# One copy of the late decays in DRAM, q and k in two 40-row transfers, narrow fillers and a new order: an mLSTM and two MoE layers on one core

## The chip, the core and the metric

The program runs on one core of a Trainium2 chip. The core has a matrix engine (TensorE: PE in the profile, its weight loads PEld), a vector engine (VectorE, DVE), an activation engine (ScalarE, ACT), a general engine (GpSimd, POOL) and a queue engine (SyncE, SP) that mostly issues DMA transfers. Each engine works through its own list of instructions in order; semaphores tie the lists together. The metric is device time in microseconds (us), the median of 3 runs.

## The reference

```python
for t in range(S):                                   # B=2, H=8, S=768, D=40
    m_new  = np.maximum(f_gate[:, :, t] + m, i_gate[:, :, t])
    f_stab = np.exp(f_gate[:, :, t] + m - m_new)
    i_stab = np.exp(i_gate[:, :, t] - m_new)
    C = f_stab * C + i_stab * outer(v_t, k_t)        # 40x40 a head
    n = f_stab * n + i_stab * k_t
    y[:, :, t] = sigmoid(o_gate_t) * (C @ q_t) / np.maximum(np.abs(n @ q_t), 1.0)
x = y as 1536 tokens of 320
xn = x / rms(x) * rms_g
x = ((silu(xn @ w_gate)) * (xn @ w_val)) @ w_out     # d_ff 1536
h = x @ w_in                                         # d_ff 2048
out = (h * np.clip(h + 3, 0, 6) / 6) @ w_out
```

## The kernel before, in words

The recurrence runs in 6 chunks of 128 steps, two halves of 64 each, for both batches at once. A chunk gives 256 tokens; two chunks make one of three groups of 512 tokens, and both MoE layers run group by group. Every matrix product of the MoE is made of split operands (a high and a low part, both fp32r), so weights are converted on the core first.

The program is written as generators of small steps, and the string `PLAN` (L774) names the order in which steps are put down: `k1.0` is a step of the load of chunk 1, batch 0; a word that comes again is the next step of the same work. Each engine's list is the order in which `PLAN` reaches its steps. The words that matter here:

- `L`, `G`, `g`: load the gates, their scans (`gates_a`), and what is made of them (`gates_b`), in two parts: chunks 0 and 1, and chunks 2 to 5.
- `B`, `b`, `d`: the decays of a chunk, spread over 128 partitions. For chunks 0 to 2 `B` does it on PE (L361, tile `fps`). For chunks 3 to 5 (the "late" ones) `gates_a` writes the decays to DRAM (tile `fsd`, L302), and `b` reads them back with every row going to 64 partitions (`gates_bc`, L347, two transfers of 256 KB a chunk, tile `fbc`). `d` is the scan on DVE (L395) that turns them into a matrix of products, one for each batch. The pool of `fbc` holds two tiles, so chunk 3 is fetched into the tile that chunk 1 frees when its `att` products are done.
- `q`, `k`: load q and k transposed (`rawqk`, L379), and k, v and the output gate (`kvo`, L386).
- `s`, `w`, `a`: scores, their weighting, and `att`, on PE, DVE and PE. `i`, `u`: products with the state, and its update. `l`, `v`, `t`: scaling of k and v, tanh of the gate. `n`, `D`, `e`, `r`: sum, denominator, output and RMS norm of a chunk. `x`: its transposition into the first MoE layer's operand `xT`.
- `W`, `c`: load and conversion of a piece of weights (six steps, spread over ACT, DVE and POOL by the table `ENGINES`). `m`, `M`, `o`: gate product, value product with its DVE and ACT work, and output product of the first MoE layer (tiles `gv` for 256 tokens, `gate` and `val` for 512). `E`, `h`, `p`, `F`: the second layer.
- `H`: a filler, one 128x512 bf16 product of ones whose result nobody reads (`warm_up`, L762).

`ON_DVE` says which of the steps that either DVE or POOL could do are on DVE.

Of the kernel before, what the change touches and what calls it, by code (L numbers as in the profile page):

```python
# [7 lines left out]
F32 = mybir.dt.float32  # L8
# [10 lines left out]
def kernel(  # L19
# [36 lines left out]
    HALF = (0, 64)  # L56
# [29 lines left out]
    hot = ap1.tile([128, 128], mybir.dt.bfloat16, name="hot")  # L86
# [4 lines left out]
    fsd = dram.tile([4, 2 * (NC - 3), BH, LS], F32, name="fsd")  # L91
# [32 lines left out]
    def dma(out, in_, eng=None):  # L124
        (eng or nc.sync).dma_start(out=out, in_=in_)
# [142 lines left out]
    def gates_a(p):  # L268
# [554 lines left out]
    h0.14 h0.15 p0.13 h0.15 h0.15 p0.14 p0.15 h1.0 F0 F0 F0 F0 F0 F0 F0 h1.1 h1.0 F0 h1.0 h1.0 h1.2
# [99 lines left out]
```

## Time and profile before

| | us |
|---|---|
| median of 3 runs | 473.79 |
| runs | 471.18, 473.79, 476.52 |
| the profiled execution, its own time | 476.52 |
| its span in the trace | 474.5 |
| PE busy / DVE busy / ACT busy / POOL busy | 449.0 / 245.2 / 216.0 / 112.4 |

The profiled execution is the slowest of the three runs. Its span is the time from the first to the last instruction in the trace, 2.0 us shorter than the time of the run. Busy PE counts fillers and products at a lowered clock in full, so 95% of busy PE isn't 95% of useful work. The trace is read by stretches below: up to the first product of the MoE at 45.66 us, from there to 148.06 us, where chunk 3 has been transposed and the next gate product starts, and the rest.

### The profile page before, as it was taken

The page shows a single profiled execution, that of the slowest core. Times are in us where ns is not written, and L with a number is a line of the kernel's source. Part 1 is how long each engine was busy: PE and PEld are TensorE (multiplying, and loading weights), DVE is VectorE, ACT ScalarE, POOL GpSimd, SP SyncE. Part 2 cuts the span into 40 slices and gives each one's busy share as a digit, 9 for nine tenths or more (in the row PEclk, how much of TensorE's full clock was granted, in tenths as well). Part 3 has the DMA queues.
Part 4 walks back from the last instruction along what each step waited for, and adds up shares of the span by engine and source line. Part 5 has one row for each costly group of instructions (what it writes and reads, how often), then busy time and mean ns, then how long its engine had stood idle before and what let it go on. Part 6 is the DMA issues. An engine that isn't in the chain of part 4 may idle for free.

```text
span 474.5 us, 9033 instructions
## 1 busy us (share of the span) xinstructions
PE 449.0 (95%) x3823; PEld 380.2 (80%) x3823; DVE 245.2 (52%) x424; ACT 216.0 (46%) x403; POOL 112.4 (24%) x112
## 2 busy tenths in 40 slices
PE   9999929979959999999999999999999999999996
PEld 4766919968848888888887788889998998899985
DVE  4778657767568573251556767863134133232312
ACT  5567736466446232232344537834244234243422
POOL 1515211125212103002151334222232121011311
PEclk9579958999978999999999999999999999999999
DMA  8942761663833010000033334310001000001001
GB/s 262 309 140 92 201 162 63 207 182 108 226 98 140 14 30 15 1 1 1 0 113 110 110 122 153 115 55 1 0 2 55 1 0 1 1 1 55 1 1 55
DMA packets 11024, 38.05 MB, mean 80 GB/s; under 512 B 1768, under 2 KB 3336, under 8 KB 10984
## 3 DMA queue, kind: packets, MB, share of 16 engines
q1 hardware_dynamic: 10408, 36.16, 25.1%
q10 hardware_dynamic: 576, 1.32, 0.8%
q8 instruction: 30, 0.49, 0.5%
q14 instruction: 10, 0.08, 0.1%
HBM read 35.41 MB, written 2.06 MB: 79 GB/s over the span
## 4 chain that ended last, share of the span: by engine, by line
PE 80%; DMA 9%; DVE 5%; ACT 2%; issue 1%; POOL 1%; SPq 0%; DVEq 0%; ACTq 0%
PE hh L593 18%; PE po L600 18%; PE gate L593 9%; PE po L687 9%; PE val L593 8%; DMA fbc<-fsd 7%; PE idle L762 5%; PE gv L593 3%; PE po L690 3%; DMA raw<-in_w_out_dram 2%; PE sc L121 2%; PE fps L361 2%; DVE fbc L395 1%; PE U L121 1%; PE inter L121 1%; PE att L121 1%
## 5 line engine op out<-in xcount | busy, mean ns | idle before, releaser
L593 PE MATMUL hh<-xT,w_in 128*128 128x512 f32 x384 | 89.4, 390 | 0.0
L600 PE MATMUL po<-w_out,g 128*128 128x320 f32 x576 | 86.4, 309 | 0.0
L600 PEld LDWEIGHTS po<-w_out,g 128*128 128x128 f32 x576 | 85.4, 188 | 0.9
L593 PEld LDWEIGHTS hh<-xT,w_in 128*128 128x128 f32 x384 | 71.6, 188 | 14.4
L593 PE MATMUL gate<-xT,w_in 128*128 128x512 f32 x240 | 60.9, 399 | 3.7 <-DVE e L648 2.9
L97 POOL TENSOR_TENSOR g<-r,g 128x512 fp32r<-128x512 f32 x27 | 35.0, 1296 | 123.2 <-ACT g L671 120.0
L668 DVE SCALAR_TENSOR_TENSOR r<-r,hh 128x512 f32<-128x512 f32 x48 | 32.8, 685 | 59.0 <-ACT r L666 59.0
L687 PE MATMUL po<-g,w_out 128*128 128x512 f32 (+1 forms) x252 | 62.6, 377 | 0.1
L593 PE MATMUL val<-xT,w_in 128*128 128x512 f32 x240 | 59.0, 391 | 0.0
L593 PEld LDWEIGHTS gate<-xT,w_in 128*128 128x128 f32 x240 | 45.6, 192 | 14.8 <-DVE e L648 3.3
L671 ACT CAST g<-r 128x512 fp32r<-128x512 f32 x48 | 29.7, 618 | 59.7 <-PE po L600 47.7
L593 PEld LDWEIGHTS val<-xT,w_in 128*128 128x128 f32 x240 | 44.7, 188 | 9.3
L687 PEld LDWEIGHTS po<-g,w_out 128*128 128x128 f32 x252 | 44.9, 198 | 8.0 <-ACT g L652 0.3
L666 ACT ACTIVATE r<-hh,three 128x512 f32<-128x512 f32 x48 | 32.9, 685 | 35.2 <-PE hh L593 26.1
L97 DVE TENSOR_TENSOR g<-r,g 128x512 fp32r<-128x512 f32 x21 | 14.5, 692 | 43.1 <-ACT g L671 43.1
L206 DVE SCALAR_TENSOR_TENSOR raw<-raw,bits 128x640 int32<-128x640 int32 x34 | 32.1, 944 | 5.0 <-ACT raw L200 4.5
L97 POOL TENSOR_TENSOR g<-e,g 128x512 fp32r<-128x512 f32 (+1 forms) x20 | 25.6, 1280 | 38.1 <-ACT g L652 38.1
L593 PEld LDWEIGHTS gv<-xT,w_in 128*128 128x128 f32 x192 | 25.2, 203 | 11.2 <-PE idle L762 9.8
L762 PE MATMUL idle<-hot 128*128 128x512 bf16 x65 | 23.6, 521 | 10.2 <-DVE g L97 9.1
L593 PE MATMUL gv<-xT,w_in 128*128 128x256 f32 x192 | 27.0, 298 | 0.8 <-ACT e L631 0.7
L690 PE MATMUL po<-g,w_out 128*128 128x512 f32 (+1 forms) x84 | 26.4, 368 | 0.0
L631 ACT ACTIVATE e<-gate 128x512 f32<-128x512 f32 x30 | 17.9, 596 | 17.1 <-PE gate L593 16.9
(129 smaller groups left out, 500.2 us busy)
## 6 DMA issues: line engine op xcount, KB each, us to landing
raw<-in_w_out_dram SPq DMA_DIRECT2D x14, 640.0 KB, 4.4
raw<-in_w_gv_dram SPq DMA_DIRECT2D x12, 640.0 KB, 8.4
rawqk<-in_qk_dram SPq DMA_DIRECT2D x12, 448.0 KB, 9.4
raw<-in_w_in_dram SPq DMA_DIRECT2D x8, 640.0 KB, 3.7
kvo<-in_kvo_dram SPq DMA_DIRECT2D x10, 484.0 KB, 4.9
out_dram<-o SPq DMA_DIRECT2D x10, 160.0 KB, 1.9
fbc<-fsd SPq DMA_DIRECT2D x6, 256.0 KB
kvo<-in_kvo_dram ACTq DMA_DIRECT2D x2, 484.0 KB
```

The source lines that it names most:

```text
L97: eng.tensor_tensor(out=out, in0=a, in1=hi.bitcast(F32), op=ALU.subtract)
L121: nc.tensor.matmul(**operands)
L206: nc.vector.scalar_tensor_tensor(out=x, in0=hw, scalar=3, in1=y, op0=ALU.logical_shift_left, op1=ALU.bitwise_or)
L593: nc.tensor.matmul(out=ps, lhsT=w[:, wk], rhs=xT[:, hl, kk], start=(n == 0), stop=(n == len(seq) - 1))
L600: nc.tensor.matmul(out=ps, lhsT=g[:, gh, ts], rhs=w[:, wh, k % 2], start=(first and n == 0), stop=(last and n == 2))
L631: nc.scalar.activation(out=e, in_=pg, func=ACTF.Silu)
L666: nc.scalar.activation(out=r, in_=ps, func=ACTF.Relu, bias=three)
L668: nc.vector.scalar_tensor_tensor(out=r, in0=r, scalar=6.0, in1=ps, op0=ALU.min, op1=ALU.mult)
L671: nc.scalar.copy(out=g[:, 0], in_=r)
L687: nc.tensor.matmul(out=ps, lhsT=w[:, at + n * 128:at + n * 128 + 128], rhs=g[:, gh], start=(first and j == 0), stop=(last and j == 2))
L690: nc.tensor.matmul(out=ps_out[gr, 2][:, ts], lhsT=w[:, 256:DM + 64], rhs=g[:, gh], start=(first and gh == 0), stop=(last and gh == 1))
L762: nc.tensor.matmul(out=idle[i].rearrange("p (a n) -> p a n", n=128), lhsT=hot, rhs=hot.unsqueeze(1).to_broadcast([128, 4, 128]), start=Tru ...
```

## The change

Four edits are made together.

1. `fsd` has one copy of the late decays and no longer four. `gates_a` writes it with one transfer, where it wrote four. `gates_bc` still makes two transfers of 64 rows of 4 KB for each chunk; the source's outermost dimension was the four copies (each read 16 times), and is now 64 repeats of one row.
2. q and k of a chunk and batch come in two transfers of 40 rows (partitions 0 to 39 and 64 to 103), where one transfer brought 112 rows, of which 32 were padding.
3. The fillers' operand `hot` has 2 columns and no longer 128; one column of it is repeated for the weights and for the moving operand.
4. `PLAN`, `ENGINES`, `ON_DVE` and `REM` are new: every step may stand elsewhere. There are 77 fillers, where there were 65. All 77 stand ahead of the first MoE product; before, two stood behind it.

```diff
-    hot = ap1.tile([128, 128], mybir.dt.bfloat16, name="hot")
+    hot = ap1.tile([128, 2], mybir.dt.bfloat16, name="hot")
-    fsd = dram.tile([4, 2 * (NC - 3), BH, LS], F32, name="fsd")
+    fsd = dram.tile([2 * (NC - 3), BH, LS], F32, name="fsd")
...
-    REM = "PAADPA"
+    REM = "APDPPD"
...
-            late_fs = fs[:, (SPREAD - PARTS[p][0]) * L:].rearrange("k (s t) -> k s t", t=LS)
-            for copy in fsd:
-                dma(copy.rearrange("s k t -> k s t"), late_fs)
+            dma(fsd.rearrange("s k t -> k s t"),
+                fs[:, (SPREAD - PARTS[p][0]) * L:].rearrange("k (s t) -> k s t", t=LS))
...
             dma(t[i * LS:(i + 1) * LS].rearrange("p b h t -> p (b h t)"),
-                fsd[:, 2 * (c - SPREAD) + i].rearrange("a k t -> a (k t)").unsqueeze(1)
-                .to_broadcast([4, LS // 4, BH * LS]))
+                fsd[2 * (c - SPREAD) + i].rearrange("k t -> (k t)").partition_broadcast(LS))
...
-        dma(r[0:qk.shape[2]].rearrange("p a h t -> p (a h t)"), qk[c, b])
+        for hh in range(2):
+            dma(r[HALF[hh]:HALF[hh] + D].rearrange("p a h t -> p (a h t)"), qk[c, b, hh])
...
-        nc.tensor.matmul(out=idle[i].rearrange("p (a n) -> p a n", n=128), lhsT=hot, rhs=hot.unsqueeze(1).to_broadcast([128, 4, 128]), start=True, stop=True)
+        nc.tensor.matmul(out=idle[i], lhsT=hot[:, 0:1].to_broadcast([128, 128]),
+                         rhs=hot[:, 0:1].to_broadcast([128, 512]), start=True, stop=True)
...
-    M0.1.0 i1 m0.1.0 c6 a1 M0.1.0 c5 M0.1.0 c6 o0.0.0 M0.1.0 n1.0 b3 n1.1 c5 b3 e1.0 m0.2.0 c6 D1 W7
+    M0.1.0 c6 o0.0.0 c7 b3 n1.1 M0.1.0 b3 n1.0 m0.2.0 W8 e1.1 c7 M0.2.0 m0.2.0 D1 m0.3.0 e1.0 M0.2.0
...
```

What the tables do is seen in the engines' lists. In the rows below a name left of the arrow is written, those right of it are read.

The first place is DVE from the sum of chunk 1 (`num<-att,num`) to the scans of chunk 3's fetched decays (`fbc<-fbc,inject`). Before:

```order
L490 TENSOR_TENSOR num<-att,num 128x328 x2
L538 SCALAR_TENSOR_TENSOR ys<-kvo,num 128x320
L496 TENSOR_SCALAR den<-num 128x16
L498 SCALAR_TENSOR_TENSOR den<-num,den 128x16
L500 RECIPROCAL den<-den 128x16
L206 SCALAR_TENSOR_TENSOR raw<-raw,bits 128x640
L538 SCALAR_TENSOR_TENSOR ys<-kvo,num 128x320
L648 TENSOR_TENSOR gv<-e,gv 128x256
L544 TENSOR_TENSOR ys<-ys,den 128x2x320
L395 SCALAR_TENSOR_TENSOR fbc<-fbc,inject 128x512 x2
```

The change, from the second row after the same sum:

```order
L206 SCALAR_TENSOR_TENSOR raw<-raw,bits 128x640
L495 TENSOR_SCALAR den<-num 128x16
L497 SCALAR_TENSOR_TENSOR den<-num,den 128x16
L499 RECIPROCAL den<-den 128x16
L537 SCALAR_TENSOR_TENSOR ys<-kvo,num 128x320
L647 TENSOR_TENSOR e<-e,gv 128x256
L543 TENSOR_TENSOR ys<-ys,den 128x2x320
L215 CAST w_in<-raw 128x640
L647 TENSOR_TENSOR gv<-e,gv 128x256
L97 TENSOR_TENSOR w_in<-raw,w_in 128x640
L97 TENSOR_TENSOR g<-gv,g 128x256
L394 SCALAR_TENSOR_TENSOR fbc<-fbc,inject 128x512
```

Four more instructions (a conversion, a value product, two differences) now stand between the sum of chunk 1 and the scan, and the second scan stands further down, behind another conversion step, a value product and two small copies.

The second place is DVE in the first stretch, from chunk 0's sum to its multiplication by the reciprocal denominator (`ys<-ys,den`). Before, that multiplication is on POOL (`L544 TENSOR_TENSOR ys<-ys,den` follows there on nothing but the denominator), and the second part's gate scan is done well ahead of this place; DVE goes on with:

```order
L500 RECIPROCAL den<-den 128x16
L443 TENSOR_TENSOR fbc<-sc,fbc 128x2x256
L395 SCALAR_TENSOR_TENSOR fbc<-fps,inject 128x512
L206 SCALAR_TENSOR_TENSOR raw<-raw,bits 128x640
L395 SCALAR_TENSOR_TENSOR fbc<-fps,inject 128x512
```

The change:

```order
L499 RECIPROCAL den<-den 128x16
L537 SCALAR_TENSOR_TENSOR ys<-kvo,num 128x320
L97 TENSOR_TENSOR w_in<-raw,w_in 128x640
L279 SCALAR_TENSOR_TENSOR fd<-fi,m_113 16x512
L281 TENSOR_TENSOR fi<-fi,m_113 16x1
L206 SCALAR_TENSOR_TENSOR raw<-raw,bits 128x640 x2
L283 TENSOR_TENSOR fi<-fi,fd 16x511
L284 TENSOR_TENSOR fi<-fi,fd 16x512
L196 TENSOR_SCALAR bits<-raw 128x640
L288 TENSOR_TENSOR fi<-fi,fd 16x512
L543 TENSOR_TENSOR ys<-ys,den 128x2x320
```

The multiplication is now on DVE, behind the second part's gate scan and its three passes, two conversion steps' `L206`, an `L196` and an `L97`.

The third place is SP's list at the first fetch. Before:

```order
L125 DMA raw<-in_w_out1_dram 128x1280
L125 DMA rawqk<-in_qk_dram 112x1024 x2
L125 DMA fbc<-fsd 64x1x1024 x2
L125 DMA raw<-in_w_gv_dram 128x1280
L125 DMA kvo<-in_kvo_dram 128x968 x2
```

The change:

```order
L125 DMA raw<-in_w_gv_dram 128x1280
L125 DMA rawqk<-in_qk_dram 40x1024 x4
L125 DMA fbc<-fsd 64x1024 x2
L125 DMA raw<-in_w_gv_dram 128x1280
L125 DMA kvo<-in_kvo_dram 128x968 x2
```

The fetch keeps its neighbours; q and k ahead of it are four transfers for two.

## Rows read from the trace of the kernel before

**Rows 1.** Windows: stretch; each engine's busy us (instructions); PE clock, DMA share, GB/s.

```profile
45.66:148.06 102.40, 84.21 (x1062) 74.54 (x1061) 72.06 (x137) 56.50 (x121) 24.39 (x25) 0.87 0.56 156
148.06:474.52 326.46, 321.21 (x1998) 278.16 (x1996) 142.17 (x232) 131.53 (x225) 71.42 (x56) 1.00 0.12 39
```

**Rows 2.** Waits of PE: for whom, us in total, times, longest.

```profile
PE idle L762 <- DVE g L97: 9.1, 1, 9.1
PE sc L121 <- issue: 4.6, 1, 4.6
PE gate L593 <- DVE e L648: 2.9, 1, 2.9
```

**Rows 3.** Chain that ended last, in order of time: start, us, what.

```profile
52.90 11.96 DMA fbc<-fsd
...
89.49 11.20 DMA fbc<-fsd
...
122.68 10.95 DMA fbc<-fsd
```

**Rows 4.** Timeline of DVE: start, us, instruction, in brackets idle time before it.

```profile
56.42 0.82 DVE L544 TENSOR_TENSOR ys<-ys,den 128x640 f32<-128x640 f32 x1
64.95 2.34 DVE L395 TENSOR_TENSOR_SCAN fbc<-fbc,inject 128x512 f32<-128x512 f32 x2 [7.71 <-DMA fbc<-fsd]
...
100.78 2.34 DVE L395 TENSOR_TENSOR_SCAN fbc<-fbc,inject 128x512 f32<-128x512 f32 x2 [1.55 <-DMA fbc<-fsd]
...
133.72 2.34 DVE L395 TENSOR_TENSOR_SCAN fbc<-fbc,inject 128x512 f32<-128x512 f32 x2 [6.07 <-DMA fbc<-fsd]
```

**Rows 5.** Windows: the three stretches at half the clock behind the waits.

```profile
61.00:74.60 13.60, 6.08 (x26) 5.50 (x26) 9.44 (x15) 5.95 (x13) 2.04 (x2) 0.50 0.49 126
105.40:108.80 3.40, 3.14 (x7) 2.48 (x8) 2.59 (x6) 2.94 (x8) 0.00 (x0) 0.50 0.87 285
139.40:146.30 6.90, 6.86 (x74) 5.71 (x75) 6.90 (x14) 4.36 (x13) 1.41 (x2) 0.50 0.49 157
```

**Rows 6.** Windows: a stretch of a fetch alone, and one of a weight load.

```profile
92.70:95.30 2.60, 2.60 (x24) 2.60 (x24) 2.15 (x7) 0.81 (x1) 0.00 (x0) 1.00 0.25 76
...
101.00:101.50 0.50, 0.50 (x4) 0.41 (x3) 0.50 (x1) 0.00 (x0) 0.00 (x0) 1.00 1.08 441
```

**Rows 7.** DMA issues: transfer, queue, count, KB each, median us to landing.

```profile
raw<-in_w_gv_dram SPq DMA_DIRECT2D x12, 640.0 KB, 8.4
...
raw<-in_w_in_dram SPq DMA_DIRECT2D x8, 640.0 KB, 3.7
```

**Rows 8.** Instructions of tile rawqk: ns min/median/max, first and last start.

```profile
L121 PE MATMUL inter<-st,rawqk x352: 227/227/248, 27.5 to 196.7; 40*64 40x41 f32 x176
...
L121 PE MATMUL inter<-zero,rawqk x32: 227/227/307, 26.7 to 27.5; 40*64 40x41 f32 x32
```

**Rows 9.** Timeline of all engines, 16 to 25 us: three rows of DVE.

```profile
16.86 1.25 DVE L279 TENSOR_TENSOR_SCAN fd<-fi,m 16x512 f32<-16x512 f32 x1
...
18.99 0.83 DVE L206 SCALAR_TENSOR_TENSOR raw<-raw,bits 128x640 int32<-128x640 int32 x1 [0.70 <-ACT raw L200]
19.74 0.67 DVE L283 TENSOR_TENSOR fi<-fi,fd 16x511 f32<-16x511 f32 x1
```

**Rows 10.** Timeline of all engines, 32.7 to 46 us: from chunk 0's multiplication on.

```profile
33.09 1.26 POOL L544 TENSOR_TENSOR ys<-ys,den 128x640 f32<-128x640 f32 x1 [9.15 <-DVE den L500]
...
35.51 0.88 SPq L125 DMA_DIRECT2D kvo<-in_kvo_dram  x2
...
39.75 0.47 ACT L410 ACTIVATE kvo<-kvo 128x320 f32<-128x320 f32 x1 [0.20 <-DMA kvo<-in_kvo_dram]
...
45.66 0.51 PE L593 MATMUL gv<-xT,w_in 128*128 128x256 f32 x2
```

**Rows 11.** Windows: two stretches without a wait for a fetch.

```profile
45.66:57.24 11.58, 11.58 (x211) 11.08 (x214) 10.05 (x22) 9.56 (x19) 2.50 (x3) 1.00 0.64 172
70.00:100.00 30.00, 29.11 (x383) 28.09 (x383) 23.73 (x50) 16.22 (x36) 5.15 (x6) 0.92 0.50 150
```

More of the change, by code (lines that the diff above doesn't have):

```diff
@@ new lines @@
+    r1 M0.2.0 M0.3.0 m0.3.0 c7 r1 m0.4.0 M0.2.0 r1 M0.3.0 k2.1 c7 M0.3.0 k3.0 M0.4.0 m0.4.0 M0.3.0
+    r1 d3.0 o0.1.0 r1 r1 c8 o0.2.0 c8 M0.4.0 x1 c8 c7 x1 d3.1 W9 M0.4.0 m0.5.0 l3.0 x1 t2.1 x1 l2.1
+    x1 o0.3.0 m0.5.0 x1 M0.4.0 x1 t3.0 M0.5.0 x1 l3.0 l3.1 c8 m0.0.1 M0.5.0 v2.1 M0.0.1 M0.5.0 c8
+    m0.0.1 c9 c9 u2 M0.0.1 c8 M0.5.0 M0.0.1 c9 m0.1.1 M0.0.1 c9 c8 M0.1.1 m0.1.1 u2 W10 c9 v3.0
+    m0.2.1 u2 c9 M0.1.1 M0.2.1 m0.2.1 m0.3.1 u2 W11 M0.2.1 u2 o0.0.1 m0.3.1 c10 c10 i2 M0.1.1 c10
+    M0.1.1 o0.4.0 i2 q4.0 i2 c10 q4.1 c11 a2 c11 M0.2.1 c10 c11 o0.5.0 b4 n2.0 c10 n2.1 b4 M0.2.1
@@ new lines @@
+    M0.3.1 e2.0 c10 m0.4.1 M0.3.1 c11 W12 M0.3.1 M0.4.1 m0.4.1 D2 c11 M0.3.1 s3 e2.1 c11 m0.5.1 w3.1
+    r2 c11 w3.0 W13 M0.5.1 m0.5.1 M0.4.1 d4.0 r2 s4 r2 k3.1 c12 k4.0 c12 o0.1.1 d4.1 l4.0 c12 o0.2.1
+    c12 M0.4.1 M0.4.1 r2 o0.3.1 M0.5.1 t3.1 v3.1 M0.5.1 c12 r2 m0.6 M0.5.1 r2 c12 t4.0 l3.1 W14
+    o0.4.1 l4.0 l4.1 m0.6 w4.0 v4.0 M0.6 w4.1 c13 c13 x2 c13 u3 u3 M0.6 c13 m0.7 M0.6 u3 M0.6 c13
+    M0.7 c14 m0.7 c14 c13 c14 u3 m0.8 M0.7 c13 M0.7 u3 W15 c14 i3 m0.8 M0.7 M0.8 i3 q5.0 i3 c14 q5.1
@@ new lines @@
+    c14 a3 M0.8 c15 c15 m0.9 c14 b5 n3.0 c15 b5 n3.1 W16 c15 x2 D3 m0.9 c15 o0.5.1 x2 e3.1 e3.0 o0.6
+    M0.8 c15 r3 W17 M0.8 o0.7 r3 r3 x2 k4.1 x2 d5.0 k5.0 M0.9 d5.1 l5.0 x2 x2 r3 o0.8 x2 r3 c16 c17
+    c16 M0.9 r3 s5 c17 c16 v4.1 M0.9 c16 m0.10 c17 M0.9 x3 c16 v5.0 c17 t5.0 t4.1 M0.10 l4.1 m0.10
+    c17 l5.1 w5.0 c16 w5.1 o0.9 M0.10 c16 c17 M0.10 W18 l5.0 x3 W19 M0.10 m0.11 x3 x3 x3 x3 x3 x3
+    o0.10 m0.11 c18 m1.0 c18 c19 c18 c19 u4 u4 m1.0 c19 c18 m1.1 c19 u4 u4 M0.11 m1.1 u4 M1.0 M0.11
@@ new lines @@
+    M0.11 M0.11 i4 M1.0 M1.0 M1.1 i4 i4 M1.0 a4 M1.1 M1.1 o0.11 n4.0 M1.1 e4.0 n4.1 m1.2 D4 E0 e4.1
+    E0 m1.3 r4 m1.2 E0 E0 r4 M1.2 E0 m1.3 k5.1 E0 r4 r4 E0 E0 M1.3 r4 E0 r4 M1.2 x4 t5.1 v5.1 M1.2
+    x4 l5.1 M1.3 o1.0 M1.2 x4 x4 x4 x4 x4 x4 m1.4 M1.3 M1.3 u5 m1.4 u5 M1.4 u5 i5 M1.4 o1.1 i5 i5
+    o1.2 M1.4 M1.4 m1.5 M1.5 m1.5 m1.6 M1.5 M1.5 M1.5 o1.3 m1.6 o1.4 M1.6 o1.5 M1.6 M1.6 M1.6 a5
+    o1.6 n5.1 n5.0 e5.1 D5 e5.0 m1.7 r5 r5 r5 M1.7 m1.7 r5 r5 r5 m1.8 M1.7 x5 M1.7 M1.7 m1.9 m1.8
+    M1.8 m1.9 m1.10 M1.8 M1.8 M1.8 M1.9 m1.10 m1.11 M1.9 M1.9 M1.9 o1.7 m1.11 M1.10 M1.11 M1.10
@@ new lines @@
+    M1.10 M1.10 x5 M1.11 o1.8 x5 x5 x5 x5 x5 x5 P o1.9 M1.11 M1.11 m2.0 m2.1 m2.0 o1.10 m2.1 o1.11
+    M2.0 E1 E1 E1 m2.2 c18 M2.0 E1 c18 M2.0 E1 E1 M2.1 m2.2 E1 M2.0 c18 E1 W20 m2.3 E1 c19 M2.1 c19
+    M2.1 o2.0 m2.3 M2.1 W21 M2.2 c20 c20 c20 c20 m2.4 M2.2 c20 M2.2 c20 c21 M2.3 M2.2 m2.4 c21 c20
+    o2.1 M2.3 W22 c21 M2.3 c21 o2.2 M2.3 c21 o2.3 c21 c22 W23 c22 M2.4 c22 c22 c22 m2.5 M2.4 c22
+    M2.4 c23 M2.4 m2.6 c22 c23 W24 m2.5 c23 M2.5 m2.6 c23 c23 m2.7 M2.5 c23 M2.5 c24 M2.6 M2.5 W25
+    c24 m2.7 c24 m2.8 c24 M2.6 c24 M2.6 o2.4 c24 m2.8 c25 c24 o2.5 c25 W26 M2.6 h0.0 c25 c25 c25
@@ new lines @@
+    c32 h0.6 h0.5 h0.4 c32 E2 c31 h0.5 h0.7 c32 c31 c32 h0.8 W33 c32 h0.9 c32 p0.0 c33 c33 c33 p0.1
+    h0.3 c33 h0.3 c33 p0.2 h0.4 c33 h0.6 h0.6 p0.3 h0.4 h0.5 h0.5 h0.7 h0.10 h0.6 h0.7 h0.8 h0.6
+    h0.8 p0.4 h0.9 h0.9 p0.5 h0.7 h0.7 p0.6 h0.8 h0.10 h0.8 h0.10 p0.7 h0.9 h0.9 p0.8 h0.10 h0.10
+    p0.9 p0.10 h0.11 h0.12 h0.11 h0.11 h0.11 h0.13 h0.12 h0.11 h0.12 h0.12 p0.11 h0.13 h0.12 h0.13
+    h0.14 h0.13 h0.13 h0.15 h0.14 h0.14 h0.14 h1.0 h0.15 h0.14 h0.15 h1.1 h1.0 h1.0 p0.12 h1.1 h1.1
+    p0.13 h0.15 h0.15 p0.14 h1.0 h1.0 p0.15 h1.1 h1.1 h1.2 F0 F0 F0 F0 F0 F0 F0 h1.3 h1.2 F0 h1.2
@@ new lines @@
+    h1.2 h1.4 h1.3 h1.2 h1.3 p1.0 h1.4 h1.4 p1.1 h1.3 h1.3 h1.5 h1.4 h1.4 h1.6 h1.5 h1.5 h1.7 h1.6
+    h1.6 h1.8 h1.7 h1.7 h1.9 h1.10 h1.11 p1.2 p1.3 h1.5 h1.5 h1.8 p1.4 h1.6 h1.8 h1.6 p1.5 h1.7 h1.9
+    h1.7 h1.9 p1.6 h1.8 h1.10 h1.8 h1.10 h1.12 h1.9 h1.11 h1.9 h1.11 h1.13 h1.12 h1.12 h1.14 h1.15
+    h2.0 p1.7 p1.8 h1.10 h1.10 h1.13 p1.9 h1.11 h1.13 h1.11 p1.10 h1.14 h1.12 h1.14 h1.12 p1.11
+    h1.13 h1.15 h1.13 h1.15 p1.12 h1.14 h2.0 h1.14 h2.0 p1.13 h1.15 h1.15 p1.14 h2.0 h2.0 p1.15 h2.1
@@ L836 @@
+    h2.15 h2.15 p2.14 h2.15 p2.15 F2 F2 F2 F2 F2 F2 F2 F2 F2
     """
@@ L897 @@
     lay = {
-        "qk": rows_qk,
+        "qk": qk.reshape(6, 2, 2, 40, 1024),
         "kvo": _np.concatenate([nat(inputs["k"]), nat(v1), og], axis=2),
```

99 lines of the change are left out of this document (28 added, 71 removed).

## The prediction, written before the changed kernel ran

> **What bounds the kernel now.** I read the stages first, then PE's waits, then the chain of waits that ended last. From 148.06 us on, PE is busy for 321.2 of 326.5 us at full clock [rows 1]: products end to end, the same set in any order, so this stretch stays as it is. Between 45.66 and 148.06 us PE is busy for only 84.2 of 102.4 us, and its mean clock is 0.87. The three large waits there, 9.1, 4.6 and 2.9 us [rows 2], look like three causes (a difference on DVE, "issue", a value product on DVE), but the chain shows one: each time it goes through the fetch of a late chunk's decays, 11.96, 11.20 and 10.95 us long [rows 3]. DVE's own list tells how that reaches PE: the scan of the fetched decays stands in line and waits 7.71, 1.55 and 6.07 us [rows 4], and the value products and differences that PE needs stand behind it. Behind each gap PE runs at half clock (0.50, the 1.2 GHz level), with 6.08, 3.14 and 6.86 us of busy time [rows 5].
>
> So the stretch holds, for these fetches: idle PE 9.4 + 2.9 + 5.2 = about 17.4 us (the waits of rows 2, with a few tenths beside them), and half of 6.1 + 3.1 + 6.9, about 8 us, lost to the clock. Without both, PE needs 102.4 - 25.4 = 77 us there. DVE is busy for 72 of the 102.4 us in the same stretch [rows 1]: it is nearly as full, and it becomes the bound once the fetches are out of the way.
>
> **The fetch, now from one copy.** Where a fetch runs alone, the 16 DMA engines are busy to a share of 0.25, at 76 GB/s; a weight load in the same kernel fills them (1.08) at 441 GB/s [rows 6]. A quarter of 16 engines is four, and the source's outermost dimension is four copies. The change makes it 64 rows. That these rows are one and the same 4 KB is what no transfer of the trace shows. Bounds: at best it is a load like others, 512 KB beside the 640 KB that land in 3.7 us when little else moves and in 8.4 us among other loads [rows 7]; at worst the sixteen engines take turns at one row, and it is as slow as before (11 us) or slower. I take 3 to 5 us from its start: it is a load of 4 KB rows from then on, and the row of weight loads is the nearest.
>
> The Trainium skill ("DMA: Bandwidth & Descriptors", section "Why a DMA increments its semaphore by 16 and not by 1") says that a transfer uses the largest number of engines, up to 16, that divides the slowest dimension of both sides. By that the fetch goes from 4 engines to 16, as the share of 0.25 bears out; by the same rule a 40-row transfer of q and k runs on 10 engines, where 112 rows ran on 16.
>
> **What waits for the fetch.** It is issued when `att` of the chunk two before is done. In the new DVE list four more instructions stand ahead of chunk 3's first scan, at some 0.4 to 0.8 us; for chunks 4 and 5 I count, from the sum behind `att` to the scan, rows that add up to 6 to 7 us by the durations of the same instructions in this trace. Before, DVE stood ready for chunk 3's scan at 64.95 - 7.71 = 57.24 us [rows 4], 4.3 us after the fetch began at 52.90 [rows 3], which is within 0.8 us of the end of `att`; for chunk 5 it was 127.65 against 122.68, 5.0 us. Now a fetch has about 6.5 us from `att`, so 5.8 from its start. At 3 to 5 us no wait is left; with the old 11 to 12 us some 5.7 us a chunk would be left.
>
> **The stretch then.** PE's floor is 77 us less 0.9 for two fillers that no longer stand there; DVE's is 72 us plus about 1.2 us that the new tables move to it (its rows between the same two products, at this trace's durations). No engine that waits on others in turn runs at 100%: in the densest stretch behind the first MoE product DVE reached 10.05 of 11.58 us, 87% [rows 11]. 73.3 / 0.87 = 84 us. I take 84 for the 102.4: **18.4 us less**. Bounds: 78 us (PE's floor and 2 of small waits) and 92 (DVE at 23.73 of 30 us, 79%, as it runs where PE is the bound [rows 11]).
>
> **The first stretch.** It gets longer. Before, chunk 0's multiplication ran on POOL for 1.26 us from 33.09, right behind the denominator; at 35.51 the load of the next k and v was issued into the buffer so freed, at 39.75 ACT took it, at 45.66 the first MoE product started [rows 10]. Now the multiplication is on DVE, behind: the second part's scan, 1.25; three passes at 0.67 and a small one at 0.15; two conversion steps at 0.83 [rows 9]; a half output, a difference and an `L196`, at about 0.5, 0.8 and 0.5; and itself 0.82 [rows 4]. That is 7.7 us, less some 0.7 that short DVE rows overlap, against 1.3 on POOL: 5.7 us later. What follows (load, tanh, transposition) is the same chain of about 10 us, but in it ACT waited before for a scan of chunk 2 and PE for 13 fillers, and the conversions done early aren't met later; I give back 2.2. So the first product starts **3.5 us later** (bounds 0 and 6).
>
> **Small ones.** q and k: 80 rows of 4 KB for 112; no wait of PE or DVE on them is in the trace, and SP's issues (24 for 12, well under 1 us each) lie where SP waits for buffers: 0. The write of the late decays: one transfer for four, 20 us ahead of its reader: 0. Fillers: 77 for 65, but PE stands ahead of DVE there, and the 0.2 us at full clock that each takes is covered by the DVE chain just counted; if that cover is gone, 12 cost 2.6 us. A repeated column costs PE nothing: a product whose moving operand is one repeated column takes 227 ns, like the one with real columns [rows 8]. The last stretch: 0.
>
> **Sum.** 45.66 + 3.5 + 84 + 326.5 = 459.7 us of span, for 474.5. A run takes 2.0 us more than its span (476.52), and this run was 2.7 us above the median of 473.79. 459.7 + 2.0 - 2.7 = **459 us**. Its own range: 450 (78 and +1) to 467 (90 and +6).
>
> **Rivals.**
> - *DVE and the first stretch take most of it.* DVE has in-order work for 73 us, and each value product stands behind conversions; a first stretch of +6 and a second of 92 us give a span of 470.1, so 469 us. For it: 79% is DVE's share over 30 us in the same stretch where next to nothing waits for a fetch. Against it: there PE was the bound, and DVE idle because of it.
> - *The fetch gains nothing.* One row is read as slowly by sixteen engines as four rows by four, 11 to 12 us. Then 5.7 us a chunk are left, 17 in all, and they eat the 18.4 - 3.5 = 14.9 that the sum gains: 476 us; with a fetch of 10 us, 471. No change, and the case in which the change doesn't do what it seems to.
> - *Slower: one engine at a time gets the row.* The place is the same scan on DVE. At 76 GB/s for four engines one moves 19 GB/s [rows 6], so 512 KB take 27 us; less 5.8, three waits are 64 us against the 14.9 gained: 523 us. It decides from where three waits outweigh 14.9, a fetch of 10.8 us, and is beyond what can be told from no change from 12.4 us up; at 14 us it is 483. Nothing in the trace speaks for it, and nothing excludes it: by the share of 0.25, each of the four copies was read by one engine.
>
> The Trainium skill ("DMA: Bandwidth & Descriptors", section "Latency and other measured facts") has a row in which streams that step through HBM in lock-step at large powers of two fall from 207 to 103 GB/s, put down to shared channels. No run here shows that. By 103 GB/s the fetch would take 5.1 us, an estimate from that page, and the forecast would stand.
>
> **How the numbers follow.** Forecast 0.64; first rival 0.16; the fetch gains nothing 0.11; slower 0.09. 1% of the median, about what a measurement can tell from no change, is 4.7 us: faster is below 469.1, slower above 478.5. Faster: the forecast, 0.64, half of the first rival, 0.08, and the edge of the second, 0.02, which is 0.74. Within 1%: the other half, 0.08, and most of the second, 0.08, so 0.16. Slower: 0.10. The range reaches from the forecast's low end over the first rival into the second: 450 to 473, leaving out some 0.18.
>
> **What would show it.** The DMA share in a fetch near 1 and no longer 0.25; a fetch of 3 to 5 us in the chain, or none; no DVE wait on `fbc<-fsd` over 1 us; no stretch at half clock between the first MoE product and chunk 3's transposition; the first `gv` product at 49 us; that transposition at about 133 and not 147 us; PE busy throughout behind it. Wrong it would be if the scans still wait 4 us and more (then the row of one copy is the brake), if DVE is idle on ACT or POOL in that stretch (then 87% was too much), or if the first product comes past 52 us.

## The result, and the profile after

The changed kernel takes **455.87 us** (median of 4 runs, 454.86 to 457.59), the kernel before 475.15 us (4 runs: the three shown above and one of 478.75): a ratio of 0.9625 (95% interval 0.9547 to 0.9703). Ratios leave out runs that are over 1.5% above the fastest of their kernel (here the one of 478.75); medians and ranges count every run. Forecast were 459 us, and 450 to 473. The profiled execution took 456.46 us, its span is 454.7, 19.8 us less than before.

The stages of the profile after; columns as in [rows 1]. 48.50 us is the first MoE product, 131.22 the moment at which ACT takes up chunk 3's transposition (148.06 before).

```profile
0.00:48.50 48.50, 43.25 (x776) 29.21 (x782) 33.35 (x62) 30.38 (x63) 16.93 (x31) 0.86 0.60 191
48.50:131.22 82.72, 78.61 (x1124) 69.74 (x1123) 74.05 (x145) 48.73 (x108) 27.64 (x24) 1.00 0.57 168
131.22:454.70 323.48, 319.01 (x1934) 277.41 (x1932) 147.55 (x239) 129.67 (x221) 63.20 (x49) 1.00 0.12 41
```

The middle stretch went from 102.40 to 82.72 us (-19.7), the first from 45.66 to 48.50 (+2.8), the last from 326.46 to 323.48 (-3.0). PE's idle time in the middle stretch fell from 18.2 to 4.1 us, and its mean clock rose from 0.87 to 1.00, so both parts of the loss that the prediction counted are gone. DVE is busy for 74.05 of 82.72 us, 90%.

PE's waits between 45 and 150 us, after; columns as in [rows 2], where the longest were 9.1, 4.6 and 2.9 us:

```profile
PE att L121 <- issue: 1.0, 1, 1.0
PE ps_al L332 <- DVE xT L582: 0.9, 1, 0.9
PE sc L121 <- DVE fbc L442: 0.8, 2, 0.5
```

DVE's scans of the fetched decays in the timeline after, which answer to [rows 4], and below them SP's issue of the third fetch:

```profile
62.43 1.23 DVE L394 TENSOR_TENSOR_SCAN fbc<-fbc,inject 128x512 f32<-128x512 f32 x1
...
89.87 1.21 DVE L394 TENSOR_TENSOR_SCAN fbc<-fbc,inject 128x512 f32<-128x512 f32 x1
...
119.74 2.34 DVE L394 TENSOR_TENSOR_SCAN fbc<-fbc,inject 128x512 f32<-128x512 f32 x2 [0.52 <-DMA fbc<-fsd]
...
113.14 1.09 SPq L125 DMA_DIRECT2D fbc<-fsd  x2
```

Two scans find their data there, the third waits 0.52 us for it. No fetch stands in the chain that ended last; before there were three of 11 to 12 us.

### The profile page after: what moved, and what is told of

It reads as the page before. It is cut to its first block, busy times and chain, and to the rows that moved or that the text cites. A ratio compares the mean times of both kernels' runs of the same rounds, so it can differ in the third digit from the quotient of the medians.

```text
span 454.7 us, 9072 instructions
## 1 busy us (share of the span) xinstructions
PE 440.9 (97%) x3829; PEld 376.4 (83%) x3835; DVE 255.0 (56%) x444; ACT 208.8 (46%) x391; POOL 107.8 (24%) x104
## 4 chain that ended last, share of the span: by engine, by line
PE 80%; DMA 7%; DVE 5%; issue 5%; ACT 2%; POOL 1%; SPq 0%; DVEq 0%; ACTq 0%; POOLq 0%
PE hh L592 19%; PE po L599 19%; PE val L592 11%; PE gate L592 11%; PE po L686 10%; DMA raw<-in_w_gv_dram 4%; PE po L689 3%; PE gv L592 3%; DMA kvo<-in_kvo_dram 3%; PE inter L121 1%; PE att L121 1%; POOL w_in L97 1%; PE ps_x L574 1%; DVE w_in L97 1%; DVE fbc L394 1%
## 5 line engine op out<-in xcount | busy, mean ns | idle before, releaser
L592 PE MATMUL gate<-xT,w_in 128*128 128x512 f32 x240 | 59.4, 392 | 0.0
L686 PE MATMUL po<-g,w_out 128*128 128x512 f32 (+1 forms) x252 | 58.7, 363 | 0.0
L97 POOL TENSOR_TENSOR g<-r,g 128x512 fp32r<-128x512 f32 x19 | 24.6, 1297 | 129.9 <-ACT g L670 128.7
L686 PEld LDWEIGHTS po<-g,w_out 128*128 128x128 f32 x252 | 42.8, 189 | 7.2
L97 DVE TENSOR_TENSOR g<-r,g 128x512 fp32r<-128x512 f32 x29 | 20.2, 697 | 46.3 <-ACT g L670 46.3
L97 POOL TENSOR_TENSOR g<-e,g 128x512 fp32r<-128x512 f32 (+1 forms) x22 | 27.0, 1227 | 64.3 <-ACT g L651 61.7
L97 POOL TENSOR_TENSOR w_in<-raw,w_in 128x640 fp32r<-128x640 f32 x13 | 22.0, 1699 | 46.4 <-ACT w_in L215 23.4
L206 DVE SCALAR_TENSOR_TENSOR raw<-raw,bits 128x640 int32<-128x640 int32 x34 | 29.3, 868 | 4.7 <-ACT raw L200 4.4
L630 ACT ACTIVATE e<-gate 128x512 f32<-128x512 f32 x30 | 17.8, 593 | 19.7 <-PE gate L592 19.7
L592 PE MATMUL gv<-xT,w_in 128*128 128x256 f32 x192 | 25.1, 286 | 0.9 <-ACT e L630 0.7
L592 PEld LDWEIGHTS gv<-xT,w_in 128*128 128x128 f32 x192 | 23.5, 191 | 1.6 <-ACT e L630 0.9
L689 PE MATMUL po<-g,w_out 128*128 128x512 f32 (+1 forms) x84 | 24.6, 359 | 0.0
```

The lines of the kernel that those rows point to most:

```text
L97: eng.tensor_tensor(out=out, in0=a, in1=hi.bitcast(F32), op=ALU.subtract)
L206: nc.vector.scalar_tensor_tensor(out=x, in0=hw, scalar=3, in1=y, op0=ALU.logical_shift_left, op1=ALU.bitwise_or)
L592: nc.tensor.matmul(out=ps, lhsT=w[:, wk], rhs=xT[:, hl, kk], start=(n == 0), stop=(n == len(seq) - 1))
L630: nc.scalar.activation(out=e, in_=pg, func=ACTF.Silu)
L686: nc.tensor.matmul(out=ps, lhsT=w[:, at + n * 128:at + n * 128 + 128], rhs=g[:, gh], start=(first and j == 0), stop=(last and j == 2))
L689: nc.tensor.matmul(out=ps_out[gr, 2][:, ts], lhsT=w[:, 256:DM + 64], rhs=g[:, gh], start=(first and gh == 0), stop=(last and gh == 1))
```

## The experiments

Each ratio is to the kernel before on the same chip (its medians there: 473.59 us for e1 to e4, 474.04 for e5 to e8, 474.48 for e9 to e11, 473.33 for e12).

| | median us | ratio, 95% interval |
|---|---|---|
| e1: old order, one copy | 458.88 | 0.9676, 0.9623 to 0.9730 |
| e2: new order, four copies | 476.98 | 1.0044, 1.0001 to 1.0086 |
| e3: four copies, outermost 16 | 458.85 | 0.9696, 0.9635 to 0.9757 |
| e4: one copy, outermost 4 | 473.19 | 0.9986, 0.9956 to 1.0017 |
| e5: the changed kernel again | 457.51 | 0.9651, 0.9616 to 0.9686 |
| e6: multiplication on POOL | 460.21 | 0.9689, 0.9640 to 0.9737 |
| e7: more PE work | 457.79 | 0.9667, 0.9627 to 0.9708 |
| e8: more DVE work | 459.19 | 0.9710, 0.9665 to 0.9755 |
| e9: small edits undone | 458.43 | 0.9695, 0.9647 to 0.9742 |
| e10: 13 fillers fewer | 461.00 | 0.9726, 0.9676 to 0.9776 |
| e11: less DVE work | 458.39 | 0.9667, 0.9607 to 0.9726 |
| e12: 21 fillers more | 462.58 | 0.9777, 0.9727 to 0.9827 |

### The fetch or the order: e1 and e2

e1 is the kernel before with the change's `fsd`, its one write and its `partition_broadcast` read. e2 is the changed kernel with the four copies back.

```diff
-                fsd[2 * (c - SPREAD) + i].rearrange("k t -> (k t)").partition_broadcast(LS))
+                fsd[:, 2 * (c - SPREAD) + i].rearrange("a k t -> a (k t)").unsqueeze(1)
+                .to_broadcast([4, LS // 4, BH * LS]))
```

> The kernel before with nothing but the one copy of the late decays: old order, old q and k, old fillers. Theory FETCH (the gain comes from the shorter fetch, the order brings little): before, DVE stood ready for the three scans 4.3, 9.7 and 5.0 us after a fetch began, so a fetch of 4 to 5 us leaves under 1 us of waiting; first MoE product at 45.7 us as before, chunk 3 transposed at 128 to 132 us, time 454 to 460 us, level with the changed kernel. Theory ORDER (the fetch was only half of it, the new order makes the rest): the three waits are gone, but PE waits for other things in the same stretch; 463 to 470 us.

> The changed kernel with the four copies back, and nothing else undone. Theory FETCH: a fetch of 11 to 12 us at a DMA share of 0.25 meets scans that are ready some 6.5 us after its start: 4 to 5.5 us of waiting at each of three scans, half clock behind them, 468 to 478 us, so no gain left. Theory ORDER: the new order covers most of a long fetch: under 2 us of waiting each, 457 to 463 us.

e1 has all of the gain, as far as can be told (0.9676 against the changed kernel's 0.9625 and, repeated, 0.9651, with intervals that overlap); e2 has none of it (1.0044). In e2's timeline DVE's first scan of each chunk waits again, for less before the first and for more before the other two than in [rows 4]:

```profile
69.61 1.23 DVE L396 TENSOR_TENSOR_SCAN fbc<-fbc,inject 128x512 f32<-128x512 f32 x1 [5.34 <-DMA fbc<-fsd]
...
103.52 1.23 DVE L396 TENSOR_TENSOR_SCAN fbc<-fbc,inject 128x512 f32<-128x512 f32 x1 [3.33 <-DMA fbc<-fsd]
...
139.84 1.22 DVE L396 TENSOR_TENSOR_SCAN fbc<-fbc,inject 128x512 f32<-128x512 f32 x1 [6.76 <-DMA fbc<-fsd]
```

15.4 us in sum, against 15.3 before: the new order alone hides nothing of a long fetch. In e1 (its profiled run was the longest of its four, 463.11 us) one such wait is left, of 1.93 us:

```profile
60.57 2.33 DVE L393 TENSOR_TENSOR_SCAN fbc<-fbc,inject 128x512 f32<-128x512 f32 x2
...
94.41 2.33 DVE L393 TENSOR_TENSOR_SCAN fbc<-fbc,inject 128x512 f32<-128x512 f32 x2
...
122.19 2.34 DVE L393 TENSOR_TENSOR_SCAN fbc<-fbc,inject 128x512 f32<-128x512 f32 x2 [1.93 <-DMA fbc<-fsd]
```

So the gain is the fetch, in either order. A share of a few microseconds for the new order is not excluded: the intervals of e1 and of the changed kernel are 0.7 to 1.6% wide.

### Engines or rows: e3 and e4

e3 has four copies and lets the 16 repeats stand outermost; e4 has the one copy and writes its 64 repeats as 4 by 16.

e3 against e2:

```diff
-                fsd[:, 2 * (c - SPREAD) + i].rearrange("a k t -> a (k t)").unsqueeze(1)
-                .to_broadcast([4, LS // 4, BH * LS]))
+                fsd[:, 2 * (c - SPREAD) + i].rearrange("a k t -> a (k t)").unsqueeze(0)
+                .to_broadcast([LS // 4, 4, BH * LS]))
```

e4 against the changed kernel:

```diff
-                fsd[2 * (c - SPREAD) + i].rearrange("k t -> (k t)").partition_broadcast(LS))
+                fsd[2 * (c - SPREAD) + i].rearrange("k t -> (k t)").unsqueeze(0).unsqueeze(0)
+                .to_broadcast([4, LS // 4, BH * LS]))
```

> The changed kernel with four copies again, but partition p reads copy p modulo 4, so the outermost dimension of the source is 16 and no longer 4. Theory ENGINES (the outermost dimension sets how many DMA engines share the fetch): as fast as in the changed kernel, some 4 to 5 us, time 454 to 458 us. Theory ROWS (how many copies of a row there are to read from decides): with four rows the fetch is clearly shorter than in the changed kernel, 3 us and less, packets under 200 ns; the time is the same all the same, as nothing waits. If it is slow, 11 us and 468 to 478 us, then what counts is neither, but four distinct rows.

> The changed kernel with its one copy, but the source written as 4 by 16 repeats of the row instead of 64. Theory ENGINES: back on four DMA engines, share 0.25, a fetch of 11 to 12 us or more (one row), 468 to 480 us. Theory ROWS: one row is read as in the changed kernel, 4 to 5 us, 454 to 458 us.

With 4 outermost the one row is as slow as the four copies were (its first fetch is 11.92 us long in e4's chain, and its scans wait 16.8 us in sum); with 16 outermost the four copies are as fast as the one. The outermost dimension decides, with one copy as with four; the number of writes does not (e3 makes four, e4 one). Windows of the four kernels, columns as in [rows 1]: the changed kernel in the second fetch, e3 in its first, e2 and e4 in their second.

```profile
83.00:84.00 1.00, 1.00 (x9) 0.84 (x8) 1.00 (x3) 0.30 (x1) 0.65 (x1) 1.00 1.12 172
84.00:85.00 1.00, 1.00 (x11) 1.00 (x10) 1.00 (x3) 0.68 (x2) 0.00 (x0) 1.00 0.95 168
```

```profile
60.00:61.00 1.00, 1.00 (x11) 1.00 (x10) 1.00 (x4) 0.00 (x0) 0.00 (x0) 1.00 0.98 311
61.00:62.00 1.00, 1.00 (x10) 1.00 (x10) 0.97 (x3) 0.38 (x1) 0.00 (x0) 1.00 1.10 288
```

```profile
94.00:95.00 1.00, 1.00 (x11) 1.00 (x10) 1.00 (x3) 0.91 (x3) 0.00 (x0) 1.00 0.29 98
```

```profile
92.00:93.00 1.00, 1.00 (x11) 1.00 (x10) 1.00 (x3) 0.70 (x3) 0.00 (x0) 1.00 0.28 90
```

The share of the last column but one is about 1 in the first two kernels and 0.28 to 0.29 in the others, about a quarter of the engines. The Trainium skill ("DMA: Bandwidth & Descriptors", section "Rules for kernel authors") says that an outermost dimension of fewer than 16, such as a leading broadcast of c copies, confines a transfer to at most c engines: e4 is that case, and its share of 0.28 agrees. The rates beside a full share, 168 to 172 GB/s from one row and 288 to 311 from four, don't show that one row is slower to read. The changed kernel again (e5, below) moves more from its one row in its second fetch:

```profile
83.00:84.00 1.00, 0.71 (x6) 0.50 (x5) 1.00 (x3) 0.91 (x2) 0.97 (x1) 1.00 0.96 311
84.00:85.00 1.00, 0.85 (x7) 0.85 (x8) 1.00 (x3) 0.31 (x2) 0.63 (x1) 1.00 1.01 238
```

In e3's window a weight load, issued at 59.91 us, may be under way too. What one row costs against four isn't shown; in both kernels the scans hardly wait.

### The first stretch: e5 and e6

e5 is the changed kernel again. e6 takes `r0` out of `ON_DVE` and moves the two squares and the load of the next k and v up in `PLAN`:

```diff
-    c5 r0 H1 H1 H1 G1 H1 G1 c5 G1 B2.0 r0 r0 k1.1 G1 T k2.0 B2.1
+    c5 r0 r0 r0 k1.1 H1 H1 H1 G1 H1 G1 c5 G1 B2.0 k2.0 G1 T B2.1
```

> The changed kernel itself, unaltered, as the measure for the other three of this call: 454 to 460 us by every theory. In its first run the half clock near the first MoE product ended at 47 us; in two of the other runs so far (old order with one copy, new order with four copies on sixteen engines) it lasted to 54 us. If that varies from run to run, this kernel shows it too, and costs up to 3.5 us.

> The changed kernel with chunk 0's multiplication by the reciprocal denominator back on POOL, and its two squares and the load behind them put down right after it. Theory CHAIN (this multiplication's place on DVE costs the first stretch its 2.9 us): load of k and v issued at 35 and not 39.6 us, first MoE product at 45.5 to 46.5 us instead of 48.5, time 1.5 to 3 us below the changed kernel. Rival: DVE and ACT have the same rest to do before the first product, which then waits for another chain: first product at 48 us, time within 1 us of the changed kernel.

The same kernel's six runs lie between 456.51 and 463.37 us, at mean clocks from 0.983 to 0.966. Where that comes from shows in windows of PE at half the clock, in the profile after and in e7's, whose list is the same up to the first MoE product:

```profile
12.40:19.20 6.80, 6.46 (x147) 5.57 (x147) 5.03 (x6) 4.03 (x10) 3.56 (x5) 0.50 1.02 284
...
42.80:46.50 3.70, 3.48 (x42) 2.52 (x44) 2.92 (x5) 2.82 (x10) 3.16 (x5) 0.54 0.76 245
```

```profile
12.00:31.90 19.90, 18.66 (x394) 14.71 (x399) 10.60 (x16) 12.21 (x24) 6.61 (x7) 0.50 0.73 217
...
45.90:55.80 9.90, 9.85 (x97) 8.96 (x97) 5.58 (x13) 5.91 (x16) 3.74 (x5) 0.50 0.46 151
```

In these two places one profile has 10.5 us at half the clock (and 3.4 more at 26.0 to 29.4 us), the other 30, and the first MoE product comes at 48.5 in the one and 50.6 us in the other (47.3 in e5, 46.6 in e8). So how much later than before it comes, 2.8 us in the profile after, differs by up to 4 us between profiles of one list. That it comes later holds in all of them: 45.7 and 46.1 us in the two profiles of the old order (before, e1), 46.6 to 50.6 in those of the new order (e6, e10 and e12, which alter this part, left aside). e6 must be set beside e7, which has the same long half clock (e6: 12.0 to 31.5 and 45.4 to 55.2 us): its first product comes at 50.7, no earlier than e7's, where 2 to 3 us were expected. The load of k and v, expected at 35 us, is issued at 41.46 us (41.57 in e7). The reason stands in e6's timeline (start, us, instruction, idle before):

```profile
33.74 1.77 POOL L543 TENSOR_TENSOR ys<-ys,den 128x640 f32<-128x640 f32 x1 [10.68 <-DVE ys L537]
34.31 2.27 DVE L279 TENSOR_TENSOR_SCAN fd<-fi,m 16x512 f32<-16x512 f32 x1
...
36.69 1.56 DVE L206 SCALAR_TENSOR_TENSOR raw<-raw,bits 128x640 int32<-128x640 int32 x2
37.55 0.80 ACT L227 CAST w_out<-raw 128x640 fp32r<-128x640 f32 x1 [4.46 <-DVE raw L206]
...
40.89 0.46 ACT L547 ACTIVATE kvo<-ys 128x321 f32<-128x321 f32 x1
```

The multiplication is done at 35.5, yet the squares (`L547`) that free the buffer start at 40.89; in e7, with the multiplication on DVE, they start at 40.91. ACT waits 4.46 us for a conversion step of DVE, which stands behind the gate scan, and the squares stand behind ACT's conversions and the exponential of the second gate part. Beside the multiplication on POOL that scan takes 2.27 us, where it takes 1.26 in e7. So the multiplication's engine is not the brake. That the scan's place on DVE is, the timeline suggests; no run moves the scan. e6 gained nothing in time (460.21 against 457.51 us, intervals overlap).

### Which engine bounds the middle stretch: e7, e8 and e11

e7, in `in1`, ahead of the gate product:

```diff
+        if N == 256:
+            extra(pg, wi1[m], 0, xT)
...
+    def extra(ps, w, u, xT):
+        for _ in range(3):
+            nc.tensor.matmul(out=ps, lhsT=w[:, 2 * u], rhs=xT[:, 0, 0], start=True, stop=True)
```

e8, in `in1_val` and in `conv`, each behind the same difference:

```diff
+        if N == 256 and low is nc.vector:
+            sub(low, g[:, 1], e, g[:, 0])
...
+            if i in (6, 7, 9, 10, 12, 13) and lo == "D":
+                sub(eng[lo], w[:, 5:10], v, w[:, 0:5])
```

e11 changes three words of `ENGINES`: piece 7 from `DDADDD` to `ADADPD`, 11 from `ADAADA` to `ADAAPA`, 13 from `DAAADD` to `AAAAPD`.

> The changed kernel with 36 more 128x256 products (three ahead of each of the 12 gate products of the first group's halves, overwritten by the real one), 0.131 us each, 4.7 us of PE time between 48.5 and 93 us. Theory DVE BOUND (my prediction's: DVE is the brake of this stretch): 0 to 2.5 us slower than the changed kernel. Theory PE BOUND (PE is busy for 78.6 of 82.7 us there): 4 to 5 us slower.

> The changed kernel with nine differences on DVE done twice (seven of a value product at 0.42 us, two of a weight piece at 0.81 us), 4.5 us of DVE time between 61 and 105 us. Theory DVE BOUND: 4 to 5 us slower than the changed kernel. Theory PE BOUND: 0 to 2 us slower, DVE's small idle times there take it up.

> The changed kernel with 3.4 us of weight conversion taken off DVE in the stretch behind the first MoE product: three differences go to POOL (0.81 us each on DVE, 1.6 on POOL), two shifts to ACT. The other direction of the run with more DVE work, which cost 1.7 us for 4.5. Theory DVE BOUND: 1.2 to 3 us less than the changed kernel (457.5 us in the last call). Theory CHAINS (no engine is the bound by itself; slower conversions make PE wait for weights): 0 to 2 us more.

By their medians 4.7 us more of PE cost 0.3 us, 4.5 us more of DVE cost 1.7; the intervals of e5, e7 and e8 overlap, so the times alone decide nothing. The profiles must be paired by clock. e8's middle stretch is at full clock throughout, as in the profile after (82.72 us, DVE 74.05). e8 first, then two more with this stretch unaltered and at full clock, e9 and e12:

```profile
46.60:133.43 86.83, 78.90 (x1124) 69.72 (x1123) 78.40 (x154) 49.09 (x108) 28.44 (x24) 1.00 0.51 160
...
49.61:134.12 84.51, 79.95 (x1127) 70.41 (x1127) 75.59 (x144) 49.18 (x108) 26.37 (x24) 1.00 0.58 175
...
53.63:138.30 84.67, 80.02 (x1127) 70.22 (x1127) 75.50 (x144) 49.01 (x108) 27.08 (x24) 1.00 0.53 166
```

e8 has 4.35 us more of DVE than the profile after, and its stretch is 4.11 longer; beside e9 and e12 it is 2.2 to 2.3 longer. e7 is paired with e6, whose stretch (50.7 to 137.4 us) is 86.7 us long and starts with the same half clock; two more unaltered stretches that start at half clock are e3's and e10's. e7, e3 and e10:

```profile
50.56:138.00 87.44, 84.38 (x1160) 76.23 (x1159) 73.39 (x145) 48.74 (x108) 26.95 (x24) 0.97 0.51 159
...
49.94:135.30 85.36, 80.66 (x1124) 71.87 (x1123) 74.17 (x145) 49.02 (x107) 29.20 (x24) 0.97 0.51 163
...
50.72:134.99 84.27, 80.53 (x1124) 71.92 (x1123) 73.51 (x144) 49.22 (x108) 27.68 (x24) 0.97 0.52 165
```

With 36 more products e7's stretch is 0.7 us longer than e6's, 2.1 longer than e3's and 3.2 longer than e10's. So work added on DVE is passed on by 2.2 to 4.1 us of 4.4, work added on PE by 0.7 to 3.2 of 4.7. That leans to DVE as the bound, as forecast, though PE is busier; unaltered stretches differ by up to 4 us among themselves (82.7 to 86.7), so it isn't shown that DVE bounds alone. e11, the other direction, didn't bear it out: 458.39 us is 0.9 above e5, where DVE BOUND expected 1.2 to 3 less and CHAINS 0 to 2 more. It doesn't settle it either. Its stretch (87.07 us, with a half clock like e5's 86.01) has 73.73 us of DVE against e5's 75.29, only 1.6 less for the 3.4 meant: `L196` on DVE takes 954 ns on average there, 664 in e5 (7 each), while POOL is busy for 31.86 us against 26.48.

### Small edits and fillers: e9, e10 and e12

e9 brings back `rows_qk` with its 112-row transfer and the 128-column `hot`. e10 leaves out the 13 fillers between `B1.1` and `a0`. e12 adds three behind each of `B0.0`, the first `g0`, `B0.1`, `B1.0`, `B2.0`, `B2.1` and the first `g1` of the second part.

A piece of e10's `PLAN`:

```diff
-    c1 H1 R l1.1 H1 u0 H1 c1 W5 H1 w0.0 c0 H1 s1
+    c1 R l1.1 u0 c1 W5 w0.0 c0 s1
```

A piece of e12's:

```diff
-    B0.0 t0.0 q1.1 g0 d0.0 B0.1 g0
+    B0.0 H1 H1 H1 t0.0 q1.1 g0 H1 H1 H1 d0.0 B0.1 H1 H1 H1 g0
```

> The changed kernel with q and k again in one 112-row transfer and the fillers' operand again 128 columns wide; copy and order stay. My prediction put both edits at 0: 455 to 460 us, within 2 us of the changed kernel (457.5 us in the last call). Rival: 32 padding rows and a transfer on more engines collide with the fetch that is issued right behind q and k; fetch over 6 us, waits at the scans of 1 us and more, 459 to 463 us.

> The changed kernel without the 13 fillers that stand between the last decays of chunk 1 and chunk 0's att products (about 16 to 28 us), 64 left of 77. Theory COVERED (my prediction's: PE stands ahead of DVE there and fillers cost nothing): first MoE product and time within 1 us of the changed kernel. Theory PE LATE (at half the clock a filler takes 0.45 us, and DVE waits 2.9 and 1.8 us for PE's scores and att): chunk 0's sum 1 to 4 us earlier, time 1 to 3 us less. Theory CLOCK (fewer fillers bring more half clock): a longer stretch at half clock, 1 to 6 us more.

> The changed kernel with 21 more fillers, three behind each group of products of 16 rows on PE (the gates' transpositions and the spreading of decays): twelve of them between 9 and 15 us, nine between 40 and 44 us. In every profile so far the clock fell to half some 4 us after PE began such a series, and the run without 13 fillers was at half clock longest and 3.5 us slower. Theory CLOCK (fillers between hold the clock): no half clock, or a much shorter one, at 12 to 24 us and at 42 to 54 us; mean clock 0.985 to 1.0 in most runs; time 452 to 456 us, less than the changed kernel's 455.9 and 457.5. Theory ONLY DELAY (the clock falls all the same): the same half clock, and 21 products in the way, at half the clock 0.45 us each ahead of DVE's scans: 459 to 466 us.

e9 is 0.9 us above e5, within their intervals, and its median time from issue to landing is 5.4 us for a fetch: the small edits are worth nothing that can be measured. e10 is 3.5 us above e5 and 2.6 above e9, with intervals that just overlap e5's and overlap e9's by far. Its six runs have mean clocks of 0.960 to 0.970, e5's 0.966 to 0.983. Its profile at half the clock:

```profile
12.00:32.00 20.00, 17.86 (x393) 14.84 (x394) 14.15 (x25) 14.04 (x26) 6.72 (x7) 0.50 0.69 217
...
43.00:56.00 13.00, 11.75 (x112) 10.10 (x110) 9.82 (x16) 6.39 (x16) 3.87 (x6) 0.50 0.31 102
```

Chunk 0's sum did come early, at 28.47 us for 31.42 in e6 with as long a half clock, so those fillers do stand in the way; with them gone the clock was low for longer, by 3 us, in the second place. Its first MoE product comes at 50.7 us, as in e6 and e7. e12 is the other extreme: the clock holds until 15.8 us and is then at half for 10.2 and 9.9 us,

```profile
9.00:15.80 6.80, 6.48 (x122) 4.65 (x119) 3.45 (x5) 3.00 (x8) 2.11 (x3) 0.99 0.94 291
15.80:26.00 10.20, 9.53 (x173) 6.36 (x173) 6.30 (x9) 4.63 (x11) 4.75 (x4) 0.51 0.81 264
...
43.50:53.40 9.90, 9.89 (x115) 6.82 (x115) 4.80 (x8) 4.32 (x15) 4.45 (x6) 0.51 0.38 119
```

and its runs' mean clocks, 0.970 to 0.988, are no lower than e5's, but the first MoE product comes at 53.6 us, behind the products in the way, and the median is 5.1 us above e5's, with intervals that don't overlap. The time is ONLY DELAY's (459 to 466), not CLOCK's. No variant beat the changed kernel.

## Why the prediction was right, and where it was off

- **One cause behind three waits, the fetch: right, and shown** by e1 and e2. The old order with the short fetch gains what the change gains, within the intervals; the new order with the long one gains nothing.
- **Four engines to sixteen by the outermost dimension: right, and shown** by e3 and e4. By the same rule q and k's 40-row transfers were to run on ten engines: from 111 to 113 us in the profile after, behind their issue and ahead of the fetch, the share is 0.61, and ten of 16 are 0.625. The size of the fetch was a little off: 3 to 5 us were taken, medians of 5.4 (e9, 4.0 to 8.2) and 6.2 us (e1, 3.8 to 8.7) from issue to landing were measured, and the third fetch of the changed kernel came 0.52 us late. Why isn't shown; a weight load is issued 1.2 us behind the first and the third fetch and shares the engines.
- **Readiness of the scans, 6.5 us behind `att`: right in the sum.** In e2 and e4 fetches of some 12 us leave waits of 15.4 and 16.8 us, where 17 were counted; the single waits are 3.3 to 6.9 us, where 5.7 were.
- **DVE as the next bound, 73.3 us at 87%: the size came out, the cause is in part argued.** Measured are 74.05 us at 90%, 82.7 us for 84. That profile has the shortest stretch of its kind: the unaltered ones of e3, e5, e6, e9, e10 and e12 take 84.3 to 86.7 us, with DVE busy for 87 to 89%. The added work of e8 and e7 leans to DVE, e11 doesn't bear it out.
- **The first stretch, +3.5: the size came out (+2.8) in part by luck, the reason isn't borne out.** The multiplication did start 4.9 us later (38.02 for 33.09) and the load behind it 4.1 us later, but e6 undid its move from POOL to DVE and got nothing back. What was left out is that ACT's squares stand behind conversions which stand behind the second part's scan. And with one list up to there this number moves by 4 us from profile to profile (46.6 to 50.6), with how long and where the clock is low.
- **The last stretch at 0: off by 3.0 us.** PE is busy 2.2 us less there, with 64 products fewer (1934 for 1998): the scores of a chunk, 1.16 us, stand ahead of the boundary now, and 0.8 us less is idle. Work moved across the line; I had taken the same set on both sides. This holds beyond one profile: the stretch takes 322.3 to 323.5 us in e3 and e5 to e12, and 326.2 in e1's old order.
- **"No stretch at half clock" behind the first MoE product: wrong as a rule.** It holds in the profile after, not in e5's, where the first three microseconds of that stretch are at half the clock, nor in e7's, where the first five are.
- **Fillers at 0: not settled.** e10, with 13 fewer, has a median 3.5 us above e5's and lower mean clocks, but the intervals overlap. That the change's 12 more brought part of the gain is not shown: e1 has the 65 and is level.
- **The rivals.** "The fetch gains nothing" and "one engine at a time" are refuted by the share near 1 and by fetches of 3.8 to 8.7 us from one row (e1, e9). "DVE and the first stretch take most of it" didn't come: 469 us were its time, and the longest of the ten runs of the changed kernel took 463.4.

Sum of the misses on the span: first stretch -0.7, middle -1.3, last -3.0, together -5.0: 454.7 for 459.7. The middle's -1.3 belongs to this profile; by the unaltered stretches of the others it would be +0.3 to +2.7.

## What to carry to other kernels

Where a replicated read is slow, look at the DMA share while it runs alone: 0.25 with a source whose outermost dimension is 4 named the cause here, and writing the broadcast with 16 (four copies) or 64 (one copy) outermost was the cure. Before a new order is credited with a gain, put the one data-path edit into the old order: here that single edit carried it, as far as the intervals tell. And where a stretch runs at a clock that differs from run to run, pair profiles by their half-clock windows before reading a difference of a few microseconds.

## What the runs showed of the hardware that was not expected

The clock fell to half while PE was busy. In the profile after, PE is busy without a gap from 9.0 us to the fall at 12.4 us, with 16-row products from 8.8 us on:

```profile
9.00:12.40 3.40, 3.40 (x92) 3.15 (x89) 2.45 (x4) 0.79 (x3) 0.91 (x1) 0.99 0.83 323
```

In e12, with 128-row fillers between those products, it fell 3.4 us later. How long it stayed low in this place was 6.8 us in that profile and 19.9 us in e7's, with the same list of products up to there, and the six times of e5 spread over 6.9 us with their mean clocks; no run here shows what sets that. The Trainium skill ("TensorE: Matmul & The Clock Gate", section "HAM oscillation — how this bites in real kernels") ties such falls to waits in which PE idles. That fits [rows 2, 5], where half clock follows each wait; the row above is a fall without one.

DVE slowed beside POOL in two places. In e6 the gate scan (`L279`) takes 2.27 us while POOL multiplies beside it, and 1.26 in e7, where POOL is idle then. In e11 an `L196` at 106.94 us takes 1.92 us beside a conversion on POOL (106.60 to 108.45); the same one in e5 takes 1.05. It doesn't hold for every pair: in the kernel before, a scan of the decays from `fps` takes 1.21 us at 33.51, beside the same multiplication. No run was made to separate these cases.
